# Batch 0's value loads without their blank rows, the softmax constant added on GpSimd, four plain float32 steps in place of five, and new due times, in a windowed attention with a gated mixing layer

## The chip, the cores and the metric

The kernel runs on one core of a Trainium2 chip. The metric is the device time of one launch in microseconds (us), the median of several runs. Engines are named as in the profile: PE multiplies matrices (TensorE, with PEld for its weight loads), DVE is VectorE, ACT is ScalarE, POOL is GpSimd, and SP (SyncE) issues nearly all DMAs. Each engine works through its own queue in order and waits on semaphores for the others.

## The reference

Inputs are q, k and v of shape (4 batches, 8 heads, 768 positions, 64) and the weights of a gated layer. Cut to what is computed:

```
scores_l = scale * q @ k^T            where |i - j| < 16, else -1e9
scores_s = scale * q @ max(k, blocks of 32) + log(32)
a = softmax(concat(scores_l, scores_s))   # sum gets + 1e-9
attn = a @ concat(v, mean(v, blocks of 32))
x = attn, heads side by side: (4, 768, 512); x_prev = x one position earlier
xk, xr = mu_k * x + (1 - mu_k) * x_prev, mu_r * x + (1 - mu_r) * x_prev
out = sigmoid(xr @ w_r) * (relu(xk @ w_k)^2 @ w_v)      # 512 -> 1024 -> 512
```

## The kernel before, in words

**Attention.** Heads are taken in pairs, so a batch has four pairs (`NPAIR`), and each pair is cut into two halves of 384 positions. One `unit` (L567) is a pair and a half. Queries are taken 64 at a time (12 windows, `NW`). A window sees 96 keys near it and the 24 block summaries: 120 columns (`NK`), in the order 64 near keys, 24 summaries (columns 64 to 87, `QW` to `KB`), 32 near keys. Scores are matmuls (L559). For each of six groups of 128 rows DVE adds the mask and finds the extreme (L585), ACT takes the exponential and the row sum (L589). DVE adds 1e-9 to the unit's six sums (L595) and takes the reciprocal (L596), and POOL multiplies the six groups by it (L601, "norm"). For batch 0 PE turns the weights round (L608) and ACT copies them out (L614). For later batches DVE and DMAs do it (L626, L635, L639). The product with the values is L656.

**Values.** `load_set` (L446) loads, for a pair, the keys (L452) and for each half a tile `vw` of 128 rows (L456): 64 rows of near values, 24 rows of zeros, 32 rows of near values, 8 rows of zeros, all laid out on the host. For batch 0, PE takes the block means out of these tiles (L490, the zero rows count for nothing in it), a second matmul puts them in place (L509), with ACT copies between (L508, L511), and the means are spread over rows 64 to 87 of both halves, by DVE or POOL (L515) and by a DMA on SP (L522). Later batches take their means by another way.

**The gated layer.** Its work per batch and half is a gate (L717 to L719, or L730 in plain float32 for the first half) and `experts` (L740), eight steps over 128 hidden features each. A step has a first product (L757), a relu and a square on ACT (L764, L766), and a second product (L784). A split step takes operands as a high and a low part, both in the fast matmul format, and adds three products: 12 matmuls of 384 columns in the first, 9 of 512 in the second. Its low and high parts come from a cast (`kh`, L770 on DVE or L771 on ACT) and a subtraction (`kl`, L772). A plain step multiplies float32 as it is: 4 matmuls and 3, each of which shows as two records. In the first half of batch 0 the first five steps are plain (`PLAIN = 5, 5`, L64), since the split weights aren't there yet. The weights are decoded from 64-bit words (L411, L414, L416) and split (L428 or L429, L433). The last batch uses a scheme with seven products in place of eight (L929, after L1020), with sums of weights (L848) that go out to memory and are fetched again.

**The order of the work.** `Plan` (L133) writes the order of every engine before the kernel runs. Each operation has a modelled length (`LENGTH`), its dependencies and a due time. `schedule` (L171) walks through time, gives each engine the ready operation that is due first, and models DMAs (`DMA_FIXED`, bytes) and the place that DVE and POOL share (`LOCKS`). Constants set the due times (`GATE0`, `STEP0`, `GATE1`, `PERIOD`, `STEP`), how far ahead things are loaded, and how PE is kept busy: where it would wait longer than `GAP`, a multiplication of zeros (`warm`, L439) is put in. The order is fixed when the kernel is built; on the chip each engine follows it and waits where the data is late. Weight combinations may not start before `AFTER` on the planner's clock.

The line that the change to the softmax sums touches is this:

```
def inverse():
    nc.vector.tensor_scalar_add(sm.t, sm.t, 1.0e-9)
    nc.vector.reciprocal(out=rc.t, in_=sm.t)
```

Of the kernel before, what the change touches and what calls it, by code (L numbers as in the profile page):

```python
# [13 lines left out]
ALU = mybir.AluOpType  # L14
# [3 lines left out]
B, H, S, D = 4, 8, 768, 64  # L18
DM, DF = 512, 1024
BLOCK, WINDOW = 32, 16  # L20
P = 128
NPAIR = H // 2
NS = S // BLOCK
QW = 64
NW = S // QW
LK = QW + 2 * WINDOW
NK = LK + NS
KB = QW + NS
KL = NW * KB + 2 * WINDOW
HW = NW // 2  # L30
NSL = HW // 2
# [8 lines left out]
LENGTH = dict(  # L40
    score=950, values2=1715, score2=1600, transpose=350, vturn=110, vpool=800, vsel=330, spread=540, spread_p=900, values=1020, gate=2740, gate32=930, e1=2100,
    e1_32=2690, e2a=1400, e2b=705, e2=705, e2_32=2600, e2l_32=930,
    warm=223, kred=865, kred2=470, kmax=90, kcopy=280, vred=865, mask=204, rc=320, evac=470, mixd=535, sub=475, khv=280,
    result=600, wbits=340, wor=610, wsub=605, tiny=60,
    exp=380, pts=375, vm=160, mixa=515, cast=405, relu=380, square=425, sigmoid=500, sigmoid3=1600, wscale=570, wcast=530,
    seven2=1040, seven4=2080, keep=375, keep_d=470, addp=600, sum=535, sum_p=900, relu2=805, relu2_d=620, result_t=500,
    tcast=530, comb3=1000, comb2=660, tsub=610, norm=345, wcast_p=640, mixa_p=600, kcopy_p=450, evac_a=375, flip=560,
)
TAIL = dict(PE=0, DVE=85, ACT=95, POOL=0, SP=0)
LATENCY = dict(PE=260, DVE=110, ACT=110, POOL=150, SP=0)  # L50
# [6 lines left out]
ATTENTION = "score", "score2", "values", "values2"  # L57
JOINED = 200
BOND = 0
DMA_FIXED = 2000  # L60
GATE0 = 32000
FULL = 34000
STEP0 = 5600
PLAIN = 5, 5  # L64
GATE1 = 80000
PERIOD = 52000
STEP = 4800
SLACK = 400
WARM = 260
WARM_END = 110000  # L70
GAP = 300
COLD = 5000
EARLY = 20000
AHEAD = 18000
ISSUE = 500
ISSUES = dict(const=0, put=460, get=400, spread=450)
HOLD = 900
LOOK = 500
LOOK_END = 60000
URGE = 5000  # L80
LOOKS = "PE",
AFTER = 100000
FLOATS = 8
AHEAD3 = 30000
SLACK3 = 200
LANES = 8
TABLE = 1300
TABLES = dict(sigmoid=1, sigmoid3=1, exp=0, wscale=0)
LOCKS = {"wbits", "wor", "wsub", "mixd", "sub", "kcopy", "khv", "spread", "sum", "tsub", "comb2", "comb3"}
FIRST = 4000  # L90
SECOND = 58000, 64000, 70000, 76000
FIRST_UNITS = 3500
FIRST_AHEAD = 14000
UNITS = 7500


class Slot:
# [35 lines left out]
class Plan:  # L133
# [10 lines left out]
    def op(self, eng, cost, due, emit, reads=(), writes=(), size=0, other=None):  # L144

        bufs = []
        for x, _ in list(reads) + list(writes):
            if isinstance(x, Buf) and x not in bufs:
                bufs.append(x)
        ways = {eng: (LENGTH.get(cost, 0), emit)}  # L150
        if other:
            ways[other[0]] = (LENGTH[other[1]], other[2])
        o = Op(len(self.ops), ways, due, bufs, size)
        for x in reads:
            o.deps.update(self.writers.get(x, ()))
        for x in writes:
            o.deps.update(self.writers.get(x, ()))
            o.deps.update(self.readers.get(x, ()))
        for x in reads:
            self.readers.setdefault(x, []).append(o)  # L160
        for x in writes:
            self.writers[x] = [o]
            self.readers[x] = []
        o.deps.discard(o)
        for x in bufs:
            x.users.append(o)
        self.ops.append(o)
        o.name = cost
        return o
# [139 lines left out]
def tile_kernel(ctx: ExitStack, tc: tile.TileContext, q, k, vT, v, consts, w_k, w_v, w_r, out):  # L309
# [136 lines left out]
    def load_set(b, p):  # L446
# [6 lines left out]
               writes=[(kt, f"k{n}")], size=P * (hi - lo) * 4)  # L453
        e["kparts"] = [(kt, f"k{n}") for n in range(len(cuts) - 1)]
        for hf in range(2):
            op("SP", "load", None, lambda hf=hf: nc.sync.dma_start(  # L456
                out=vw[hf].t[:, 0:S], in_=v[b, p, hf]),
               writes=[(vw[hf], "a"), (vw[hf], "b")], size=P * HW * 512)

        def blocks():  # L460
            return kt.t[:, 0:NW * KB].rearrange("p (j c) -> p j c", c=KB)
# [21 lines left out]
        if b == 0:  # L483
            tp = buf("mm", F32, False)

            def means():
                for i in range(3):
                    for g in range(4):
                        w = 3 * g + i
                        nc.tensor.matmul(  # L490
                            tp.t[32 * g:32 * g + 32, 0:P], pool_sb[:, 4 - 2 * i:36 - 2 * i],
                            windows(vw[w // HW])[:, w % HW, :], start=(i == 0), stop=(i == 2))

            op("PE", "vpool", None, means, reads=[(x, y) for x in vw for y in "ab"] + [*POOLM], writes=[(tp, 0)])
        else:
            vt, vs, vb, far = buf("st", U32), buf("vs"), buf("vb"), buf("farv")

            def tokens():
                return vt.t[:, 0:S].bitcast(F32)

            op("SP", "load", None, lambda: nc.sync.dma_start(out=tokens(), in_=vT[b - 1, p]), writes=[(vt, 0)], size=P * S * 4)
            op("DVE", "vred", None, lambda: nc.vector.tensor_reduce(
                out=vs.t[:, 0:NS], in_=tokens().rearrange("p (n c) -> p n c", c=BLOCK), op=ALU.add, axis=AX.X),
               reads=[(vt, 0)], writes=[(vs, 0)])
            op("DVE", "vturn", None, lambda: nc.vector.transpose(out=vb.t, in_=vs.t), reads=[(vs, 0)], writes=[(vb, 0)])
# [61 lines left out]
    def unit(b, p, hf, e, due):  # L567
# [23 lines left out]
                    accum_out=sm.t[:, NSL * h + i:NSL * h + i + 1]),  # L591
                   reads=[(y[h], i), (mn[h], i)], writes=[(y[h], i), (sm, NSL * h + i)])

        def inverse():
            nc.vector.tensor_scalar_add(sm.t, sm.t, 1.0e-9)  # L595
            nc.vector.reciprocal(out=rc.t, in_=sm.t)  # L596

        op("DVE", "rc", None, inverse, reads=[(sm, n) for n in range(2 * NSL)], writes=[(rc, 0)])
        for h in range(2):
            for i in range(NSL):  # L600
                op("POOL", "norm", None, lambda h=h, i=i: nc.gpsimd.tensor_scalar(  # L601
# [39 lines left out]
               reads=[(far, c) for c in range(4)], writes=spots, size=P * 3072)  # L641

        parts = e.setdefault("parts", [])
        parts.append((av, vw, pts, [(vw, x) for x in "ab"] + spots, hf))
        if b > 0 and hf == 0:
            return
        todo = list(parts)
# [555 lines left out]
```

## Time and profile before

| | |
|---|---|
| median of 3 runs | 418.39 us (418.35 to 419.38) |
| the profiled execution | 419.9 us, span of the core 417.9 us |
| granted clock of TensorE | 1.00 |
| DMA | 79.68 MB, 191 GB/s on the mean |
| first PE instruction to last | 0.99 to 414.6 us |

The span runs from the first instruction of the program to its last. A busy PE in these records isn't PE at its peak, since matmuls overlap and their ends are modelled; the pace is read from one start to the next, which the chain of work does. The time goes to the slowest engine of each stage, so the busy times are read by stretches.

### The profile page before, as it was taken

To read this page: it belongs to the slowest core of one execution; us is meant where nothing else is said; L and a number is where in the kernel's file an instruction comes from. 1 tells how busy PE (TensorE), PEld (TensorE's weight loads), DVE (VectorE), ACT (ScalarE), POOL (GpSimd) and SP (SyncE) were. 2 spreads that over 40 slices of the span, in tenths; PEclk is the share of its full clock that TensorE was granted. 3 is DMA by queue.
4 is the path that set the end of the run, shared out by engine and by line. 5 is a ranking of instruction groups with operands and counts; after the bars stand their busy time and mean duration, and the time that the engine had idled before them with its cause. 6 is when DMAs were issued, how large, how long until landed. Compare 5 with 4: busy or idle time off the path is not lost.

```text
span 417.9 us, 9808 instructions
## 1 busy us (share of the span) xinstructions
PE 411.0 (98%) x3363; PEld 349.6 (84%) x3363; DVE 344.6 (82%) x1053; ACT 286.8 (69%) x815; POOL 126.2 (30%) x255
## 2 busy tenths in 40 slices
PE   9999999999999999999999999999999999999996
PEld 8754556788888888988888889988889899999996
DVE  3879999999998699879798779569476598878993
ACT  2889999899874589537774459465595675669710
POOL 0471565534660033602353000422433030204100
PEclk9999999999999999999999999999999999999999
DMA  8995678678877585787735554486855314230012
GB/s 306 405 292 208 221 257 313 236 252 235 241 204 236 168 279 173 226 274 240 234 106 155 179 163 190 114 315 190 243 166 138 107 66 146 67 103 25 2 57 94
DMA packets 48193, 79.68 MB, mean 191 GB/s; under 512 B 6736, under 2 KB 28176, under 8 KB 48144
## 3 DMA queue, kind: packets, MB, share of 16 engines
q1 hardware_dynamic: 48000, 78.78, 58.3%
q8 instruction: 26, 0.43, 0.4%
q10 hardware_dynamic: 144, 0.28, 0.2%
q14 instruction: 23, 0.19, 0.2%
HBM read 58.68 MB, written 20.07 MB: 188 GB/s over the span
## 4 chain that ended last, share of the span: by engine, by line
PE 74%; ACT 9%; DVE 8%; DMA 5%; issue 2%; POOL 0%; SPq 0%; ACTq 0%; DVEq 0%; POOLq 0%
PE bank L784 20%; PE bank L757 19%; PE bank L929 14%; PE bank L1020 4%; PE bank L656 4%; PE bank L559 4%; ACT y L589 3%; DMA kt<-in_k 3%; PE bank L440 3%; PE bank L719 2%; PE bank L717 2%; PE bank L718 2%; DMA st<-in_w_k 2%; DVE wc L848 1%; DMA farw<-wc 1%
## 5 line engine op out<-in xcount | busy, mean ns | idle before, releaser
L601 POOL TENSOR_SCALAR y<-y,rc 128x120 f32<-128x120 f32 x192 | 93.8, 509 | 129.8 <-DVE mn L585 48.9
L757 PE MATMUL bank<-xs,w 128*128 128x384 f32 x556 | 112.0, 349 | 0.7 <-ACT z L708 0.5
L757 PEld LDWEIGHTS bank<-xs,w 128*128 128x128 f32 x556 | 98.1, 188 | 9.5 <-issue 1.0
L589 ACT ACTIVATE y<-y,mn 128x120 f32<-128x120 f32 x192 | 73.4, 385 | 15.3 <-DVE mn L585 15.0
L784 PE MATMUL bank<-w,kh 128*128 128x512 f32 x258 | 69.5, 397 | 0.4 <-DVE kh L770 0.4
L764 ACT ACTIVATE r<-bank 128x384 f32<-128x384 f32 x48 | 23.5, 490 | 50.2 <-PE bank L757 49.9
L784 PEld LDWEIGHTS bank<-w,kh 128*128 128x128 f32 x258 | 47.2, 188 | 9.5 <-DVE kh L770 0.7
L585 DVE CUSTOM_DVE_ANT_0 y<-bank,consts_sb 128x120 f32<-128x120 f32 x192 | 41.9, 272 | 0.1
L784 PE MATMUL bank<-w,kl 128*128 128x512 f32 x129 | 39.4, 398 | 0.0
L589 ACT ACTIVATION_READ_ACCUMULATOR y<-y,mn 128x1 f32 x192 | 36.4, 189 | 0.0
L656 PEld LDWEIGHTS bank<-pts,vx 120*64 120x64 f32 x768 | 24.0, 138 | 8.3 <-issue 6.8
L929 PE MATMUL bank<-xs,w 128*128 128x384 f32 x126 | 30.8, 337 | 0.0
L626 DVE STREAM_TRANSPOSE st<-y 128x384 f32<-128x384 f32 x48 | 27.0, 566 | 3.4 <-POOL y L601 2.8
L784 PEld LDWEIGHTS bank<-w,kl 128*128 128x128 f32 x129 | 23.8, 188 | 5.9 <-DVE kl L772 0.3
L770 DVE CAST kh<-r 128x384 fp32r<-128x384 f32 x26 | 9.7, 372 | 22.6 <-ACT r L766 22.6
L685 POOL TENSOR_SCALAR xa<-vx,om_sb 128x384 f32<-128x384 f32 x11 | 9.1, 832 | 62.6 <-DVE xs L699 62.6
L656 PE MATMUL bank<-pts,vx 120*64 120x64 f32 x768 | 26.8, 224 | 0.0
L772 DVE TENSOR_TENSOR kl<-r,kh 128x384 fp32r<-128x384 f32 x43 | 24.3, 565 | 2.2 <-ACT kh L771 0.8
L766 ACT ACTIVATE r<-r 128x384 f32<-128x384 f32 x48 | 25.3, 527 | 0.7
L559 PEld LDWEIGHTS bank<-kt,qt 64*64 64x64 f32 x768 | 19.9, 133 | 6.5 <-issue 3.4
L559 PE MATMUL bank<-kt,qt 64*64 64x120 f32 x768 | 24.7, 268 | 0.4 <-DVE kt L478 0.3
L697 ACT CAST xs<-xa 128x384 fp32r<-128x384 f32 x40 | 20.0, 510 | 6.9 <-DVE xa L688 6.9
(374 smaller groups left out, 832.2 us busy)
## 6 DMA issues: line engine op xcount, KB each, us to landing
vx<-in_v SPq DMA_DIRECT2D x32, 384.0 KB
far<-st SPq DMA_DIRECT2D x96, 96.0 KB
pts<-far SPq DMA_DIRECT2D x24, 384.0 KB
kt<-in_k SPq DMA_DIRECT2D x15, 544.0 KB
qt<-in_q SPq DMA_DIRECT2D x32, 192.0 KB
st<-in_vT SPq DMA_DIRECT2D x12, 384.0 KB
out<-z SPq DMA_DIRECT2D x18, 256.0 KB
st<-in_w_k SPq DMA_DIRECT2D x8, 512.0 KB
```

The source lines that it names most:

```text
L559: nc.tensor.matmul(cells(to[h])[cs, i, 0:NK], t.t[hs, n * QW:(n + 1) * QW], kt.t[hs, w * KB:w * KB + NK], start=True, stop=True)
L585: op("DVE", "mask", None, lambda h=h, i=i, var=var: nc.vector.tensor_tensor_reduce(out=cells(y[h])[:, i, 0:NK], in0=cells(spot[h])[:, i, 0 ...
L589: op("ACT", "exp", None, lambda h=h, i=i: nc.scalar.activation(cells(y[h])[:, i, 0:NK], cells(y[h])[:, i, 0:NK], AF.Exp, bias=mn[h].t[:, i ...
L601: op("POOL", "norm", None, lambda h=h, i=i: nc.gpsimd.tensor_scalar(out=cells(y[h])[:, i, 0:NK], in0=cells(y[h])[:, i, 0:NK], scalar1=rc.t ...
L626: op("DVE", "flip", due - (FIRST_AHEAD if b == 1 else AHEAD) + 8000 + 600 * h, lambda h=h: nc.vector.transpose(out=turned()[:, :, h], in_= ...
L656: nc.tensor.matmul(av.t[hs, w * QW:(w + 1) * QW], windows(vw)[:, w, hs], weights_of(pts)[0:NK, 2 * c:2 * c + 2, h, i], start=True, stop=True)
L757: nc.tensor.matmul(ps.t[:, 0:HT], w.t[:, p * P:(p + 1) * P], x[p][s].t, start=(n == 0), stop=(n == len(terms) * NPAIR - 1))
L764: op("ACT", "relu", None, lambda: nc.scalar.activation(r.t, ps.t[:, 0:HT], AF.Relu), reads=[(ps, 0)], writes=[(r, 0)])
L766: op("ACT", "square", None, lambda: nc.scalar.activation(r.t, r.t, AF.Square), reads=[(r, 0)], writes=[(r, 0)])
L772: op("DVE", "sub", None, lambda: nc.vector.tensor_tensor(out=kl.t, in0=r.t, in1=kh.t.bitcast(F32), op=ALU.subtract), reads=[(r, 0), (kh, 0 ...
L784: nc.tensor.matmul(acc[t].t, a.t[:, t * P:(t + 1) * P], v.bitcast(F32) if single else v, start=start, stop=stop)
L929: nc.tensor.matmul(bank.t[:, 0:HT], pair[w].t[:, col:col + P], a[k][s].t, start=(first and n == 0), stop=(n == 3 * nk - 1), skip_group_che ...
```

## The change

Four things are done together. First, for batch 0 the value loads leave out the 24 zero rows and the last 8: each half's load becomes two DMAs, of rows 0 to 63 and 88 to 119, and POOL writes zeros to rows 64 to 87 at the very start, since the block means still read them. The regions of the tile are now three ("a", "b", "c"). Later batches load as before. Second, adding 1e-9 to the softmax sums becomes an operation of its own on POOL ("eps"); DVE keeps the reciprocal. Third, `PLAIN` goes from 5, 5 to 4, 4: the fifth step of the first half is a split one, so its two weight tiles must be split before it, and the tile whose second-product weights are split last is the fourth. Fourth, some thirty constants of the planner change: due times, assumed DMA time, how far it looks ahead and on which engines, when zeros are multiplied, and when the weight combinations may start.

```diff
--- before.py
+++ after.py
@@ -40,11 +40,11 @@
 LENGTH = dict(
     score=950, values2=1715, score2=1600, transpose=350, vturn=110, vpool=800, vsel=330, spread=540, spread_p=900, values=1020, gate=2740, gate32=930, e1=2100,
     e1_32=2690, e2a=1400, e2b=705, e2=705, e2_32=2600, e2l_32=930,
-    warm=223, kred=865, kred2=470, kmax=90, kcopy=280, vred=865, mask=204, rc=320, evac=470, mixd=535, sub=475, khv=280,
+    warm=223, kred=865, kred2=470, kmax=90, kcopy=280, vred=865, mask=204, rc=160, eps=110, evac=470, mixd=535, sub=475, khv=280,
     result=600, wbits=340, wor=610, wsub=605, tiny=60,
     exp=380, pts=375, vm=160, mixa=515, cast=405, relu=380, square=425, sigmoid=500, sigmoid3=1600, wscale=570, wcast=530,
     seven2=1040, seven4=2080, keep=375, keep_d=470, addp=600, sum=535, sum_p=900, relu2=805, relu2_d=620, result_t=500,
-    tcast=530, comb3=1000, comb2=660, tsub=610, norm=345, wcast_p=640, mixa_p=600, kcopy_p=450, evac_a=375, flip=560,
+    tcast=530, comb3=1000, comb2=660, tsub=610, norm=345, blank=700, wcast_p=640, mixa_p=600, kcopy_p=450, evac_a=375, flip=560,
 )
 TAIL = dict(PE=0, DVE=85, ACT=95, POOL=0, SP=0)
 LATENCY = dict(PE=260, DVE=110, ACT=110, POOL=150, SP=0)
@@ -57,41 +57,41 @@
 ATTENTION = "score", "score2", "values", "values2"
 JOINED = 200
 BOND = 0
-DMA_FIXED = 2000
+DMA_FIXED = 2300
 GATE0 = 32000
 FULL = 34000
-STEP0 = 5600
-PLAIN = 5, 5
-GATE1 = 80000
-PERIOD = 52000
-STEP = 4800
-SLACK = 400
+STEP0 = 4400
+PLAIN = 4, 4
+GATE1 = 76000
+PERIOD = 51000
+STEP = 4400
+SLACK = 800
 WARM = 260
 WARM_END = 110000
-GAP = 300
+GAP = 500
 COLD = 5000
 EARLY = 20000
 AHEAD = 18000
 ISSUE = 500
 ISSUES = dict(const=0, put=460, get=400, spread=450)
-HOLD = 900
-LOOK = 500
-LOOK_END = 60000
-URGE = 5000
-LOOKS = "PE",
-AFTER = 100000
+HOLD = 600
+LOOK = 1000
+LOOK_END = 34000
+URGE = 2000
+LOOKS = "PE", "DVE", "ACT", "POOL"
+AFTER = 150000
 FLOATS = 8
-AHEAD3 = 30000
-SLACK3 = 200
+AHEAD3 = 20000
+SLACK3 = 100
 LANES = 8
 TABLE = 1300
 TABLES = dict(sigmoid=1, sigmoid3=1, exp=0, wscale=0)
 LOCKS = {"wbits", "wor", "wsub", "mixd", "sub", "kcopy", "khv", "spread", "sum", "tsub", "comb2", "comb3"}
-FIRST = 4000
+FIRST = 4500
 SECOND = 58000, 64000, 70000, 76000
-FIRST_UNITS = 3500
-FIRST_AHEAD = 14000
-UNITS = 7500
+FIRST_UNITS = 2500
+FIRST_AHEAD = 12000
+UNITS = 6500
 
 
 class Slot:
@@ -453,9 +453,16 @@
                writes=[(kt, f"k{n}")], size=P * (hi - lo) * 4)
         e["kparts"] = [(kt, f"k{n}") for n in range(len(cuts) - 1)]
         for hf in range(2):
+            if b == 0:
+                op("POOL", "blank", -1.0e5, lambda hf=hf: nc.gpsimd.memset(vw[hf].t[QW:KB, 0:S], 0.0), writes=[(vw[hf], "b")])
+                for part, lo, hi in ("a", 0, QW), ("c", KB, NK):
+                    op("SP", "load", None, lambda hf=hf, lo=lo, hi=hi: nc.sync.dma_start(
+                        out=vw[hf].t[lo:hi, 0:S], in_=v[b, p, hf, lo:hi]),
+                       writes=[(vw[hf], part)], size=(hi - lo) * HW * 512)
+                continue
             op("SP", "load", None, lambda hf=hf: nc.sync.dma_start(
                 out=vw[hf].t[:, 0:S], in_=v[b, p, hf]),
-               writes=[(vw[hf], "a"), (vw[hf], "b")], size=P * HW * 512)
+               writes=[(vw[hf], "a"), (vw[hf], "b"), (vw[hf], "c")], size=P * HW * 512)
 
         def blocks():
             return kt.t[:, 0:NW * KB].rearrange("p (j c) -> p j c", c=KB)
@@ -491,7 +498,7 @@
                             tp.t[32 * g:32 * g + 32, 0:P], pool_sb[:, 4 - 2 * i:36 - 2 * i],
                             windows(vw[w // HW])[:, w % HW, :], start=(i == 0), stop=(i == 2))
 
-            op("PE", "vpool", None, means, reads=[(x, y) for x in vw for y in "ab"] + [*POOLM], writes=[(tp, 0)])
+            op("PE", "vpool", None, means, reads=[(x, y) for x in vw for y in "abc"] + [*POOLM], writes=[(tp, 0)])
         else:
             vt, vs, vb, far = buf("st", U32), buf("vs"), buf("vb"), buf("farv")
 
@@ -591,11 +598,10 @@
                     accum_out=sm.t[:, NSL * h + i:NSL * h + i + 1]),
                    reads=[(y[h], i), (mn[h], i)], writes=[(y[h], i), (sm, NSL * h + i)])
 
-        def inverse():
-            nc.vector.tensor_scalar_add(sm.t, sm.t, 1.0e-9)
-            nc.vector.reciprocal(out=rc.t, in_=sm.t)
-
-        op("DVE", "rc", None, inverse, reads=[(sm, n) for n in range(2 * NSL)], writes=[(rc, 0)])
+        sums = [(sm, n) for n in range(2 * NSL)]
+        op("POOL", "eps", None, lambda: nc.gpsimd.tensor_scalar(
+            out=sm.t, in0=sm.t, scalar1=1.0e-9, scalar2=1.0, op0=ALU.add, op1=ALU.mult), reads=sums, writes=sums)
+        op("DVE", "rc", None, lambda: nc.vector.reciprocal(out=rc.t, in_=sm.t), reads=sums, writes=[(rc, 0)])
         for h in range(2):
             for i in range(NSL):
                 op("POOL", "norm", None, lambda h=h, i=i: nc.gpsimd.tensor_scalar(
@@ -641,7 +647,7 @@
                reads=[(far, c) for c in range(4)], writes=spots, size=P * 3072)
 
         parts = e.setdefault("parts", [])
-        parts.append((av, vw, pts, [(vw, x) for x in "ab"] + spots, hf))
+        parts.append((av, vw, pts, [(vw, x) for x in "abc"] + spots, hf))
         if b > 0 and hf == 0:
             return
         todo = list(parts)
```

## The prediction

> **What bounds the kernel now.** I read the page first, for the busy time of each engine, then the busy time by stages, because the averages hide that the stages have different limits.
>
> ```profile
> span 417.9 us, 9808 instructions
> PE 411.0 (98%) x3363; PEld 349.6 (84%) x3363; DVE 344.6 (82%) x1053; ACT 286.8 (69%) x815; POOL 126.2 (30%) x255
> vx<-in_v SPq DMA_DIRECT2D x32, 384.0 KB
> ```
>
> ```profile
> 8.00:20.00 12.00, 11.70 (x207) 9.20 (x199) 10.19 (x57) 9.68 (x40) 4.24 (x14) 1.00 1.03 406
> 20.00:30.00 10.00, 9.55 (x120) 5.46 (x120) 8.22 (x28) 8.25 (x30) 7.17 (x13) 1.00 0.97 298
> 30.00:40.00 10.00, 9.58 (x69) 4.67 (x68) 8.91 (x20) 9.14 (x19) 2.25 (x3) 1.00 0.71 259
> 40.00:60.00 20.00, 19.64 (x124) 10.93 (x124) 19.53 (x56) 19.94 (x54) 11.96 (x14) 1.00 0.58 204
> 60.00:110.00 50.00, 49.49 (x462) 37.77 (x462) 48.92 (x187) 47.00 (x150) 22.43 (x49) 1.00 0.83 266
> 110.00:160.00 50.00, 49.50 (x454) 42.66 (x458) 43.55 (x144) 33.82 (x105) 18.46 (x37) 1.00 0.69 210
> 160.00:340.00 180.00, 180.00 (x1481) 158.02 (x1474) 141.46 (x450) 116.62 (x336) 49.41 (x106) 1.00 0.59 185
> 340.00:417.90 77.90, 74.56 (x425) 74.06 (x423) 62.08 (x115) 41.08 (x89) 9.52 (x10) 1.00 0.23 75
> ```
>
> The columns are the stretch, its length, then PE, PEld, DVE, ACT and POOL busy, the granted clock (1.00 throughout), the busy share of the DMA engines and GB/s. PE is the bound: from 160 to 340 us it is busy 180.00 of 180.00. But its busy time holds filler. The timeline of PE shows it at the start (L440 multiplies zeros by zeros and gives nothing):
>
> ```profile
> 0.99 6.61 PE L440 MATMUL bank<-zero_sb 128*128 128x128 f32 x32 [0.99 <-POOL zero_sb L1066]
> 7.53 0.85 PE L559 MATMUL bank<-kt,qt 64*64 64x120 f32 x24
> 8.31 2.50 PE L440 MATMUL bank<-zero_sb 128*128 128x128 f32 x20
> ...
> 12.30 0.94 PE L440 MATMUL bank<-zero_sb 128*128 128x128 f32 x6
> ...
> 13.88 0.83 PE L440 MATMUL bank<-zero_sb 128*128 128x128 f32 x6
> ...
> 19.51 0.49 PE L440 MATMUL bank<-zero_sb 128*128 128x128 f32 x2
> ```
>
> So four kinds of PE time can shrink. Work: steps that can be made cheaper. Filler: 6.61 us before the first scores, and 2.50 + 0.94 + 0.83 + 0.49 = 4.8 us after them. Idle time between 8 and 160 us: 0.30 + 0.45 + 0.42 + 0.36 + 0.51 + 0.50 = 2.5 us. And the tail: in the last row 77.90 - 74.56 = 3.3 us, which no edit touches. Beyond the work, then, 4.8 + 2.5 = 7.3 us can be won at the very most once the scores have begun. DVE and ACT are nearly full from 40 to 110 us (19.53 and 19.94 of 20, 48.92 and 47.00 of 50); there a later DVE is a later PE.
>
> **Four plain steps in place of five.** The chain of work that ended last has both kinds of step:
>
> ```profile
> 52.72 2.58 PE bank L784 x6
> ...
> 62.93 2.58 PE bank L757 x8
> ...
> 167.55 2.10 PE bank L757 x12
> 169.65 2.08 PE bank L784 x9
> ```
>
> A plain float32 step is 2.58 us (first matrix, 4 matmuls of two records) and 2.58 us (second). A split step is 2.10 and 2.08. The fifth step changes kind: 5.16 - 4.18 = **-0.98 us** of PE work, which counts in full, since PE has nothing to hide it behind. Its price lies on DVE and ACT:
>
> ```profile
> L433 DVE TENSOR_TENSOR w<-w,w 128x512 fp32r<-128x512 f32 x19 | 13.7, 733 | 0.0
> L770 DVE CAST kh<-r 128x384 fp32r<-128x384 f32 x26 | 9.7, 372 | 22.6 <-ACT r L766 22.6
> L772 DVE TENSOR_TENSOR kl<-r,kh 128x384 fp32r<-128x384 f32 x43 | 24.3, 565 | 2.2 <-ACT kh L771 0.8
> L595 DVE TENSOR_SCALAR sm<-sm 128x6 f32<-128x6 f32 x32 | 5.3, 167 | 3.0 <-ACT y L589 2.8
> L596 DVE RECIPROCAL rc<-sm 128x6 f32<-128x6 f32 x32 | 6.1, 192 | 1.1
> ```
>
> New work is one kh and one kl: 0.37 + 0.57 = 0.94 us of DVE. The two splits of the fifth weight tiles (L433, 2 x 0.73 us, and their casts) are no new work, they only come some steps sooner, in the stage where DVE is full. What hides this is the saving of the next part; without it, up to 0.94 + 1.47 = 2.4 us would be late at PE's fifth step.
>
> **The constant on GpSimd.** L595 leaves DVE. The timeline of DVE shows what one costs, and the pair of units to which the second rival below refers:
>
> ```profile
> 6.14 0.31 DVE L478 COPY kt<-ks 128x288 f32<-128x288 f32 x1
> ...
> 11.63 0.17 DVE L595 TENSOR_SCALAR sm<-sm 128x6 f32<-128x6 f32 x1 [1.04 <-ACT y L589]
> 11.84 0.19 DVE L596 RECIPROCAL rc<-sm 128x6 f32<-128x6 f32 x1
> ...
> 43.54 0.15 DVE L595 TENSOR_SCALAR sm<-sm 128x6 f32<-128x6 f32 x1
> ...
> 89.86 0.16 DVE L595 TENSOR_SCALAR sm<-sm 128x6 f32<-128x6 f32 x1
> ...
> 91.70 0.26 DVE L595 TENSOR_SCALAR sm<-sm 128x6 f32<-128x6 f32 x1
> ...
> 107.82 0.17 DVE L595 TENSOR_SCALAR sm<-sm 128x6 f32<-128x6 f32 x1
> ```
>
> From its start to that of the reciprocal it is 11.84 - 11.63 = 0.21 us, 32 times: 6.7 us off DVE in all. Nine of the 32 lie between 40 and 110 us, the first at 43.54 and the last at 107.82: 1.9 us, twice the 0.94 that the fifth step adds. The eps goes from ACT to POOL to DVE to POOL where it went ACT, DVE, DVE, POOL. On POOL it costs between the smallest memset and a norm over 120 columns:
>
> ```profile
> 0.73 0.20 POOL L1066 MEMSET zero_sb<- 128x128 f32 x1 [0.29 <-POOLq L1191]
> 0.87 0.11 POOL L1068 MEMSET vs<- 128x8 f32 x1
> ...
> 12.22 2.08 POOL L601 TENSOR_SCALAR y<-y,rc 128x120 f32<-128x120 f32 x6 [10.97 <-DVE mn L585]
> ```
>
> That is 0.11 to 2.08 / 6 = 0.35 us; I take 0.15, since six columns are nearest to the 128x8 row. The new wait is DVE's: its reciprocal now waits for POOL, and behind it in DVE's queue stand the masks, kl and xs that ACT and PE want. In time for PE I take **-0.3 us**, out of the 0.36 + 0.51 us idle from 40 to 110; the bounds are -0.9 and, as a rival, plus.
>
> **Batch 0's values.** Each of the 8 loads moves 96 rows of 128 and becomes two DMAs. From 8 to 20 us the DMA engines are full at 406 GB/s, so a load of 384 KB takes 0.97 us and by its bytes would take 0.73: 8 x 0.24 = 1.9 us less queue when the last has landed. The nearest row is the load itself, as its rows keep their length. The far end comes from the one narrow copy at the front, 24 rows, 72 KB:
>
> ```profile
> L522 SPq DMA_DIRECT2D vx<-vm x4: 822/827/972, 17.6 to 31.4; - x4
> ```
>
> In the stretch from 20 to 30 us, which holds most of them, the engines are just as full but move 298 GB/s: 1.08 MB less than at 406, or 2.7 us, so 0.67 us for each even if all four lay there, where their bytes would make 0.18. Were each of the two new pieces to take as long as a whole load, the queue would be 8 x 0.97 = 7.8 us later. I take -1.9 for the queue. Little of it can reach PE: in SP's order of issues the keys and queries of pairs 0 and 1 come ahead of any value; the keys of pair 2 stand behind two of these loads (-0.5), those of pair 3 behind four (-1.0), the last weights behind all. With 4.8 us of filler to draw on, I count half, **-1.0 us** (0 to -1.9).
>
> The Trainium skill speaks against this edit: SBUF — State Buffer, section "Door 1: The DMA port swizzle", has a transfer over partitions 0 to 63 reach 8 of 16 ports, at 196 GB/s where 128 partitions got 328. By its figures a pair of pieces would be an estimated 1.5 us instead of 0.97, the queue 4 us later and not 1.9 sooner. By that rule, the 24-row copies (0.67 us or more for 72 KB) agree in direction, but their pieces are short; no row has a 64-partition load.
>
> The eight extra issues cost SP about 0.43 us each (3.4 us before 20 us):
>
> ```profile
> L456 SPq DMA_DIRECT2D vx<-in_v x32: 327/430/1222, 3.1 to 303.6; - x32
> ```
>
> I cost them at nothing: what stands behind them on SP's queue, keys, queries and gate weights, would join a full DMA queue. The eight memsets of 24 x 768 go first on POOL. By the two memset rows (0.20 us for 128 columns, 0.11 for 8) a column is 0.75 ns, so one is about 0.68 us, all 5.5 us, over at about 6.5. POOL's next work is at 12.22, so that hides them; should they hold DVE's L478 of 6.14 to 6.45 until 6.5, the first scores at 7.53 still have a microsecond in hand.
>
> **New due times.** They change the order on all queues. PE's work is the same in any order; what can go is waiting. From 160 to 340 us there is none. Delaying the weight combinations (AFTER) takes DVE work out of 110 to 150 us, where PE was idle 0.50 us, and puts it after 150, where DVE has 38 of 180 us free. I take **-0.3 us**; the bounds are -1.9 (the 2.2 us of idle time from 20 to 160 us but for the 0.3 counted above) and a few us more, as any reordering can make a new wait.
>
> **The sum.** -0.98 - 1.0 - 0.3 - 0.3 = -2.6 us. The profiled execution took 419.9 us for a span of 417.9, so 417.3 for it; the median, 418.39, lies 1.5 below that execution, which gives **415.8 us** (0.6% faster). About 0.3%, or 1.26 us, is what a measurement of this kernel can tell from no change: 417.1 to 419.7.
>
> **The rivals.** First, that only the work counts: the filler and the waits stay because ACT and DVE, at 9.68 and 10.19 of 12 us in the stage from 8 to 20, set the front and not the DMA. Then -0.98 remains: 417.4, no change that can be told. For it speaks that the first scores start straight after filler, not after a wait.
>
> Second, the slower side by the loads: narrow pieces at half the rate. A 64-row piece takes what 128 rows take, 0.97 us, a 32-row piece 0.48: 0.48 more for each load, 3.9 us at the end of the eight. Pair 3's values, then its mix and the last gate products wait; PE has 0.45 + 0.42 us of idle time from 20 to 40 that this would replace, so 3.0 us come on top of -0.98 - 0.6: 419.8. It is slower by over 0.3% from about 0.46 us more for each load. The short 24-row copies are all in the trace that supports it. This is what the Trainium skill's rule above would do.
>
> Third, DVE waits for the eps. In a pair of units such as that of 89.86 and 91.70 us the second eps may stand behind the first unit's six norms on POOL:
>
> ```profile
> L601 POOL TENSOR_SCALAR y<-y,rc 128x120 f32<-128x120 f32 x192 | 93.8, 509 | 129.8 <-DVE mn L585 48.9
> POOL y L601 <- DVE rc L596: 42.2, 12, 11.1
> ```
>
> Six take 6 x 0.509 = 3.05 us, the units are 1.84 apart, so DVE would wait 1.2 us, in the four pairs of batch 1 where DVE is full 4.9 us: 418.39 - 0.98 - 1.0 + 4.9 = 421.3. Against it: POOL itself mostly sits waiting for the reciprocal (42.2 us in 12 waits), so the eps usually finds it free.
>
> **How the numbers follow.** Forecast 0.64, only the work 0.20, narrow loads 0.09, queued eps 0.07. The forecast's low end takes the whole 1.9 of the queue and all 2.5 us of idle time: 418.39 - 0.98 - 1.9 - 2.5 = 413.0. The range reaches up past the narrow loads to 420.0 and leaves out the queued eps. Faster 0.64, same 0.20, slower 0.09 + 0.07 = 0.16.
>
> **What would show it.** The plain steps: L757 in pieces x8 four times, not five. The loads: the stage from 8 to 20 us still at about 400 GB/s, gate weights landing 1 to 2 us sooner, filler after 8 us below 4 us; a rate near 300 GB/s there means the narrow loads. The eps: DVE's reciprocal with no wait for POOL over 0.3 us, DVE's busy time down by about 4 us (5.3 less 0.94). PE's idle time from 20 to 160 us at or below 2.2 us. A single new PE wait of over 2 us in any stage, or 3 us more filler, would make the forecast wrong.

## The result and the profile after

Slower, and outside the range on the other side: 423.68 us (421.22 to 425.93, 6 runs) against 418.72 us (418.35 to 419.47, 6 runs), a ratio of 1.011 with a 95% interval of 1.007 to 1.015. The profiled execution of after took 421.99 us, 2.1 us more than that of before (419.9) and less than most of the timed runs of after; that spread is taken up again below.

The page of after, its span, engines and the DMA issues of the values:

```profile
span 419.9 us, 9858 instructions
PE 408.8 (97%) x3362; PEld 349.7 (83%) x3362; DVE 335.6 (80%) x1020; ACT 288.2 (69%) x818; POOL 137.4 (33%) x297
...
vx<-in_v SPq DMA_DIRECT2D x24, 384.0 KB
...
vx<-in_v SPq DMA_DIRECT2D x8, 192.0 KB
vx<-in_v SPq DMA_DIRECT2D x8, 96.0 KB
```

Batch 0's eight loads have become 8 of 192 KB and 8 of 96 KB, as the change says. VectorE (DVE) has 9.0 us less to do and GpSimd (POOL) 11.2 us more. TensorE (PE) is busy 2.2 us less and the span is 2.0 us longer, so it waits more. The stages show where (columns as in the prediction: busy time of PE, PEld, DVE, ACT, POOL, then granted clock, DMA share, GB/s):

```profile
8.00:20.00 12.00, 8.75 (x148) 6.58 (x148) 7.88 (x44) 5.99 (x29) 3.46 (x11) 1.00 1.04 275
20.00:30.00 10.00, 8.81 (x117) 5.42 (x115) 7.02 (x30) 8.02 (x33) 5.11 (x13) 1.00 1.05 247
30.00:40.00 10.00, 9.04 (x95) 4.74 (x94) 7.49 (x14) 8.13 (x17) 7.12 (x12) 1.00 0.91 296
40.00:60.00 20.00, 19.67 (x118) 10.12 (x117) 19.62 (x57) 19.86 (x53) 8.66 (x11) 1.00 0.64 222
60.00:110.00 50.00, 49.23 (x454) 39.14 (x453) 46.84 (x159) 42.72 (x128) 24.65 (x48) 1.00 0.76 254
```

From 8 to 20 us the DMA engines are as full as before (1.04) and move 275 GB/s where they moved 406. PE is busy 8.75 of 12 us where it was 11.70, DVE 7.88 where it was 10.19, ACT 5.99 where it was 9.68: everyone waits for data. From 8 to 40 us PE is now idle 3.25 + 1.19 + 0.96 = 5.4 us where it was 0.30 + 0.45 + 0.42 = 1.2. PE's timeline at the front and its waits name what is late:

```profile
8.70 0.84 PE L566 MATMUL bank<-kt,qt 64*64 64x120 f32 x24 [0.98 <-DVE kg L477]
9.47 1.16 PE L440 MATMUL bank<-zero_sb 128*128 128x128 f32 x8
11.23 1.18 PE L497 MATMUL bank<-vx,consts_sb 120*32 120x128 f32 x24 [0.60 <-DMA vx<-in_v]
12.34 0.94 PE L440 MATMUL bank<-zero_sb 128*128 128x128 f32 x6
14.51 0.85 PE L566 MATMUL bank<-kt,qt 64*64 64x120 f32 x24 [1.24 <-DVE kg L477]
...
16.38 1.25 PE L497 MATMUL bank<-vx,consts_sb 120*32 120x128 f32 x24 [0.69 <-DMA vx<-in_v]
...
22.74 0.38 PE L497 MATMUL bank<-vx,consts_sb 120*32 120x128 f32 x3 [0.78 <-DMA vx<-in_v]
```

The block means (L497, L490 before) wait for values three times. The scores (L566) wait twice, and the view names VectorE's work on keys (L477) for it; but the second of these runs until 14.56 us, past the start of the scores at 14.51. The semaphores of the trace have the queries of these scores land at 8.56 and 14.42 us, just before they start. In the kernel with whole loads of the first experiment below the same queries land at 7.49 and 11.33. In the order of both kernels the second pair's queries stand behind the first pair's values. What PE lost from 0 to 40 us (the time between starts less the usual pace of that work, filler of zeros counted as lost) rose from 14.9 to 19.3 us, +4.4. After 40 us it fell by 1.5, and the work itself by 1.0; together that is +1.9, and the span is 2.0 longer.

The mean of 275 GB/s hides two rates. This is the view of DMA over 4 to 30 us, in 40 slices of 0.65 us, first of after, then of a kernel that differs from it only in loading whole tiles again (the first experiment):

```profile
GB/s 397 345 368 354 319 189 217 264 225 226 364 367 207 182 235 252 247 345 335 414 396 303 195 180 233 266 273 384 336 210 202 241 225 262 251 235 225 165 150 289
```

```profile
GB/s 429 417 380 394 428 402 443 410 391 398 392 416 433 427 382 408 382 387 399 406 410 399 394 395 416 418 395 372 272 179 216 321 162 91 202 422 365 143 192 347
```

After's row falls again and again to between 180 and 230 and comes back to some 350 to 400 in between; the other stays near 400 until 22 us. The valleys are where the values pass: in steps of 0.2 us in which nothing but values moved, the trace has 185 to 231 GB/s in after and 395 to 417 with whole loads. The last of batch 0's values landed at 29.5 us in after, at 25.6 in before and at 24.75 in the kernel with whole loads.

### The profile page after: what moved, and what is told of

It is laid out like the page before. It is cut to its first block, busy times and chain, and to the rows that moved or that the text cites. A ratio compares the mean times of both kernels' runs of the same rounds, so it can differ in the third digit from the quotient of the medians.

```text
span 419.9 us, 9858 instructions
## 1 busy us (share of the span) xinstructions
PE 408.8 (97%) x3362; PEld 349.7 (83%) x3362; DVE 335.6 (80%) x1020; ACT 288.2 (69%) x818; POOL 137.4 (33%) x297
## 4 chain that ended last, share of the span: by engine, by line
PE 77%; DMA 9%; ACT 6%; DVE 5%; issue 1%; SPq 1%; DVEq 0%; ACTq 0%
PE bank L790 22%; PE bank L763 21%; PE bank L935 14%; PE bank L662 4%; PE bank L1026 4%; PE bank L566 3%; PE bank L723 3%; PE bank L724 3%; PE bank L725 3%; DMA st<-in_w_r 2%; ACT y L596 2%; DMA vx<-in_v 2%; DMA kt<-in_k 2%; DMA st<-in_w_k 1%; DMA qt<-in_q 1%
## 5 line engine op out<-in xcount | busy, mean ns | idle before, releaser
L607 POOL TENSOR_SCALAR y<-y,rc 128x120 f32<-128x120 f32 x192 | 91.7, 496 | 21.6 <-DVE rc L604 15.3
L790 PE MATMUL bank<-w,kh 128*128 128x512 f32 x264 | 71.4, 398 | 0.8 <-DVE kh L776 0.8
L790 PEld LDWEIGHTS bank<-w,kh 128*128 128x128 f32 x264 | 48.1, 188 | 10.7 <-DVE kh L776 1.0
L602 POOL TENSOR_SCALAR sm<-sm 128x6 f32<-128x6 f32 x32 | 8.8, 276 | 111.6 <-ACT y L596 109.7
L632 DVE STREAM_TRANSPOSE st<-y 128x384 f32<-128x384 f32 x48 | 27.2, 570 | 10.3 <-POOL y L607 10.3
L566 PEld LDWEIGHTS bank<-kt,qt 64*64 64x64 f32 x768 | 19.8, 133 | 8.5 <-issue 3.1
L566 PE MATMUL bank<-kt,qt 64*64 64x120 f32 x768 | 24.3, 268 | 2.2 <-DVE kg L477 2.2
L473 DVE TENSOR_REDUCE kg<-kt 128x48 f32<-128x768 f32 (+1 forms) x17 | 15.3, 899 | 13.9 <-DMA kt<-in_k 13.8
```

Of the source, the lines that this page charges most:

```text
L566: nc.tensor.matmul(cells(to[h])[cs, i, 0:NK], t.t[hs, n * QW:(n + 1) * QW], kt.t[hs, w * KB:w * KB + NK], start=True, stop=True)
L632: op("DVE", "flip", due - (FIRST_AHEAD if b == 1 else AHEAD) + 8000 + 600 * h, lambda h=h: nc.vector.transpose(out=turned()[:, :, h], in_= ...
L790: nc.tensor.matmul(acc[t].t, a.t[:, t * P:(t + 1) * P], v.bitcast(F32) if single else v, start=start, stop=stop)
```

## The experiments

**One: after with whole loads (whole_in_after).** The order on every queue stays that of after; only the loads are whole again, and the memsets are gone.

```diff
-op("POOL", "blank", ..., lambda hf=hf: nc.gpsimd.memset(vw[hf].t[QW:KB, 0:S], 0.0), ...)
+op("POOL", "blank", ..., lambda: None, ...)
-    nc.sync.dma_start(out=vw[hf].t[lo:hi, 0:S], in_=v[b, p, hf, lo:hi]),   # parts "a" and "c"
+    part == "a" and nc.sync.dma_start(out=vw[hf].t[:, 0:S], in_=v[b, p, hf]),
```

> The changed kernel in its own order on every queue, but each of batch 0's eight value loads is one DMA of all 128 rows again and the eight memsets are gone. Theory (loads that span part of the partitions move at about half the rate): from 8 to 20 us the DMA engines return from 275 to about 400 GB/s, PE's idle time from 8 to 40 us falls from 5.4 us to under 2.5, and the time falls by 3 to 5 us, to 419 to 420. Rival (the new due times made the front late, as the first scores' queries now stand behind the next pair's keys; the loads matter little): still slower than before by 1%, 423, first scores still at about 8.7 us and idle time still over 4 us.

Measured: 417.16 us, ratio to before 0.994 (0.991 to 0.996), the fastest kernel of the study. The time is lower than expected (419 to 420). So the loads and their memsets cost after about 1.7%, and the rest of the change, in this order, gains 0.6%. No run has the memsets without the split loads, so their own share stays open. Its front:

```profile
8.00:20.00 12.00, 9.88 (x179) 7.53 (x177) 9.29 (x53) 7.71 (x37) 5.13 (x14) 1.00 1.04 405
20.00:30.00 10.00, 9.22 (x129) 5.26 (x129) 7.95 (x26) 9.46 (x32) 6.82 (x16) 1.00 0.87 276
30.00:40.00 10.00, 10.00 (x90) 5.18 (x86) 9.06 (x23) 8.83 (x19) 5.40 (x7) 1.00 0.87 281
```

405 GB/s again, and PE idle 2.9 us from 8 to 40 where after has 5.4; under 2.5 was expected.

**Two: the loads alone, in before (narrow_in_before).** Before's order, each of batch 0's value loads as rows 0 to 63 and 88 to 119, the eight memsets at the start.

```diff
+def values_in(hf=hf):
+    for lo, hi in ((0, QW), (KB, NK)) if b == 0 else ((0, P),):
+        nc.sync.dma_start(out=vw[hf].t[lo:hi, 0:S], in_=v[b, p, hf, lo:hi])
```

> The kernel before in its own order, but each of batch 0's value loads is two DMAs of rows 0 to 63 and 88 to 119 and the rows between are set to zero by eight memsets at the start. Theory: 8 to 20 us at about 280 GB/s, the last value load lands about 4 us later, time 421 to 423. Rival (due times): 417 to 418.7, since fewer bytes are moved.

Measured: 424.32 us (419.78 to 427.81), ratio 1.013 (1.010 to 1.017). Without the two longest of the six runs the median is 423.96, 1.0% above before. The loads and memsets alone cost in before's order about what all of after costs. The profiled execution was the fastest of the six (419.78); even there the stage from 8 to 20 us ran at 313 GB/s, and the last value landed 2.2 us later than in before, where about 280 GB/s and 4 us were expected.

**Three and four: two loads of 128 rows, or two of 64 (two_by_columns, two_by_rows).** Both double the number of value loads of batch 0 in before and leave the bytes as they are. One cuts each load by columns, the other by rows.

```diff
+for lo, hi in ((0, HT), (HT, S)):                 # two_by_columns
+    nc.sync.dma_start(out=vw[hf].t[:, lo:hi], in_=v[b, p, hf, :, lo:hi])
+for lo, hi in ((0, QW), (QW, P)):                 # two_by_rows
+    nc.sync.dma_start(out=vw[hf].t[lo:hi, 0:S], in_=v[b, p, hf, lo:hi])
```

> The kernel before, with each of batch 0's value loads cut into two DMAs by columns: 128 rows each, half the row. Same bytes, eight more DMAs. Theory (the span of partitions counts): as before, 418.0 to 419.0, 8 to 20 us at 390 GB/s or more. Rival (each DMA has its cost, whatever its shape): slower like the narrow loads, 421 or more, rate about 300 GB/s.

> The kernel before, with each of batch 0's value loads cut into two DMAs by rows: 0 to 63 and 64 to 127. Same bytes, eight more DMAs, no memsets. Theory: each half takes about as long as the whole did (0.97 us), so the queue is up to 7.8 us later after the eight, 8 to 20 us at 230 to 260 GB/s, time 423 to 427. Rival (bytes and number of DMAs count): the same as the cut by columns.

Measured: 419.70 us, ratio 1.000 (0.998 to 1.002), and 427.48 us, ratio 1.018 (1.015 to 1.022). The stage from 8 to 20 us, by columns and then by rows:

```profile
8.00:20.00 12.00, 10.15 (x173) 7.82 (x175) 9.41 (x55) 8.56 (x37) 4.24 (x14) 1.00 1.05 396
```

```profile
8.00:20.00 12.00, 9.19 (x143) 6.88 (x143) 6.84 (x44) 7.40 (x34) 4.24 (x14) 1.00 1.04 290
```

The same bytes in as many pieces run at 396 or at 290 GB/s, by how many partitions a piece spans (230 to 260 was expected for the cut by rows). Neither the number of issues nor a fixed cost of each piece can be the cause. This is the rule of the Trainium skill that the prediction cited against the edit. Another section of the same page of the Trainium skill (SBUF — State Buffer, "Can I just issue two DMAs to hit both halves?") says that a transfer below partition 64 and one above it run one after the other and hardly side by side. Two_by_rows agrees with it: its last values landed at 34.4 us, those of two_by_columns at 27.2.

**Five: zeros where PE waits (zeros_in_after).** After's timed runs lie up to 4 us above its profiled one, and several show a granted clock of 0.992 to 0.996. I thought that PE, idle at the front, loses its clock in most runs. This kernel puts 20 more multiplications of zeros into PE's queue, at the five waits shown above and ahead of one more score.

```diff
+for _ in range(3 if p in (1, 2) else 0):          # ahead of the block means
+    nc.tensor.matmul(tp.t[:, 512 - P:512], zero_sb, zero_sb, start=True, stop=True)
+for _ in range(extra.get(o, 0)):                  # 4 ahead of three scores, 2 ahead of the first means
+    o.emit()                                      # o: a multiplication of zeros
```

> The kernel after, with some 18 more multiplications of zeros at the front of TensorE's queue, at the five places where it waited for batch 0's keys and values (0.6 to 1.2 us each). They can't make any data come sooner. Theory A, the idle TensorE at the front costs granted clock in most runs, and that makes up what the timed runs lie above the profiled one (421.2 to 425.9 us at 0.992 to 1.000): the clock is 0.999 or 1.000 in every run, the runs lie within 1.5 us of each other, and the median is near 421.5. Theory B, the late data alone do it: the clock may rise, but the median stays at 423 to 424.5 and the runs spread over 4 us.

Measured: 425.32 us (421.01 to 428.33). The clock was 0.999 or 1.000 in five of six runs, and the time was no shorter and no steadier. My theory of the clock fell. Its profiled execution took 425.46 us at a clock of 0.999, and shows what differs:

```profile
8.00:20.00 12.00, 10.05 (x147) 8.31 (x146) 7.18 (x36) 5.66 (x28) 2.57 (x8) 1.00 1.05 261
20.00:30.00 10.00, 8.85 (x128) 5.98 (x126) 6.25 (x34) 4.64 (x19) 5.76 (x15) 1.00 1.01 220
```

261 and 220 GB/s, where the profiled execution of after had 275 and 247; PE's busy time there is padded by the zeros, DVE and ACT show the waiting. Across the profiled executions time goes with the landing of the last of batch 0's values:

| kernel | last value landed, us | profiled execution, us |
|---|---|---|
| whole_in_after | 24.75 | 417.6 |
| before | 25.6 | 419.9 |
| two_by_columns | 27.2 | 419.8 |
| narrow_in_before | 27.8 | 419.8 |
| after | 29.5 | 422.0 |
| zeros_in_after | 32.0 | 425.5 |
| two_by_rows | 34.4 | 428.3 |

Each row is one execution, and two orders are mixed here. In before's order (before, two_by_columns, narrow_in_before, two_by_rows) a landing up to 27.8 us costs nothing that shows, and the 6.6 us from there to two_by_rows cost 8.5, of which up to 1.7 are a fall of PE's clock (last section). In after's order the first 4.7 us already cost 4.4, and the next 2.5 cost 3.5. That the loads' rate varies from run to run and makes the spread of after is what this table suggests; the timed runs have no trace to show it.

**Six to nine: the other edits, each with an order of its own.** Each of these is a kernel in which the planner writes the order anew.

```diff
+PLAIN = 4, 4                          # plain4_only: before with this alone
+op("POOL", "eps", ...); rc=160, eps=110   # eps_only: before with the constant on GpSimd, its lengths
+op("SP", "load", ..., size=P * HW * 512)   # all_but_loads: after with before's value loads
+PLAIN = 5, 5; GATE1 = 76000; ...      # due_times_only: before with after's other constants
```

> The kernel before with four plain steps in place of five and nothing else changed; the planner writes its order anew with the old constants. Theory (the work term counts in full): 0.98 us less PE work, ratio 0.9965 to 0.9985, PE's idle time from 40 to 110 us within 0.5 us of the 0.87 of before. Rival (DVE, full from 40 to 110 us, gives it back): ratio 0.9985 or more, idle time there over 1.5 us.

> The kernel before with the constant of the softmax sums on GpSimd and nothing else changed. Theory (hidden): ratio 0.997 to 1.001, DVE's busy time down by 5 us. Rival (DVE waits for the eps behind other norms): ratio over 1.003 and waits of PE on DVE of over 1 us between 40 and 160 us.

> The changed kernel without its edit of the value loads: one DMA of 128 rows each, no memsets; eps, four plain steps and the new constants stay, and the planner writes the order anew. Theory (narrow loads are the whole loss): ratio 0.990 to 0.996, rate from 8 to 20 us about 400 GB/s, no run with a granted clock under 0.996. Rival (the new order is fragile at the front in itself): ratio 0.999 or more.

> The kernel before with the new planner constants alone: five plain steps, whole loads, the sums as before. Theory (the order after the front got better, PE's lost time after 40 us fell by 1.5 us in the changed kernel): ratio 0.994 to 0.998. Rival (my forecast of -0.3 us): 0.998 to 1.001. Third (queries behind keys cost a microsecond at the start): over 1.001, first scores after 8 us.

| kernel | median, us | ratio, 95% |
|---|---|---|
| plain4_only | 425.81 | 1.015 (1.013 to 1.018) |
| eps_only | 431.42 | 1.028 (1.025 to 1.031) |
| all_but_loads | 426.58 | 1.017 (1.014 to 1.020) |
| due_times_only | 418.98 | 0.999 (0.997 to 1.000) |

I had not expected the first three; the fourth fits the forecast for the due times, no change that can be told. All_but_loads does the very work of whole_in_after; only the order differs, since the planner counted whole loads in the one and narrow ones in the other. (The order includes which of two engines takes some of the copies, and how many multiplications of zeros are put in.) The order alone is worth 2.4%, 9 us, more than any edit here. Where 4.4 of the 9 us go, first all_but_loads, then whole_in_after:

```profile
100.00:110.00 10.00, 8.49 (x109) 7.51 (x102) 7.71 (x42) 8.14 (x33) 4.47 (x12) 1.00 0.72 185
...
160.00:340.00 180.00, 176.56 (x1461) 153.21 (x1461) 143.89 (x456) 119.49 (x341) 55.77 (x127) 1.00 0.64 195
```

```profile
100.00:110.00 10.00, 9.46 (x91) 8.56 (x90) 8.10 (x46) 9.99 (x43) 6.28 (x17) 1.00 0.78 208
...
160.00:340.00 180.00, 180.00 (x1445) 158.35 (x1444) 146.30 (x452) 122.67 (x346) 48.89 (x114) 1.00 0.65 197
```

PE waits at the handover to batch 1 and, in all_but_loads, it waits 3.4 us in the long stage where before and whole_in_after have no wait at all. Plain4_only loses at the same handover; its PE there, line numbers as in before:

```profile
102.19 0.97 PE L757 MATMUL bank<-xs,w 128*128 128x384 f32 x4 [0.85 <-ACT xs L697]
...
109.60 1.66 PE L784 MATMUL bank<-w,kh 128*128 128x512 f32 x6 [1.20 <-ACT kh L771]
...
114.19 0.92 PE L656 MATMUL bank<-pts,vx 120*64 120x64 f32 x24 [0.82 <-DVE mn L585]
```

Step after step waits a little for ACT or DVE, which are busy 9.87 and 9.76 of the 10 us from 100 to 110.

**Ten to sixteen: the edit or the order?** Two kernels move the constant and keep the order: to GpSimd in before, and back to VectorE in whole_in_after.

```diff
-nc.vector.tensor_scalar_add(sm.t, sm.t, 1.0e-9)                      # eps_in_order; eps_back reverses it
+nc.gpsimd.tensor_scalar(out=sm.t, in0=sm.t, scalar1=1.0e-9, scalar2=1.0, op0=ALU.add, op1=ALU.mult)
```

> The kernel before with its own written order on every queue; only the 32 additions of the constant go from VectorE to GpSimd, each just ahead of where the reciprocal stood. Theory A, the move by itself costs nothing that counts (a GpSimd step of about 0.25 us off the path, 32 x 0.167 us off VectorE): 418.0 to 419.5, ratio 0.998 to 1.001, and the 2.8% that the same edit cost with a rewritten order came from the order. Theory B, the forecast's gain: 417.7 to 418.1 or less. Theory C, the second rival on the slower side (VectorE waits behind GpSimd's six norms): over 421, with VectorE's reciprocal waiting over 1 us in the pairs of units.

> The kernel after in its own order with whole value loads (416.0 to 418.7 us, ratio 0.994), and the addition of the constant back on VectorE at the place that the order gives it. If the move is worth nothing, the ratio stays at 0.992 to 0.996. If the move carries the gain of that order (VectorE is full from 40 to 110 us), it goes up to 0.997 or more. If the move costs in that order (the added wait of VectorE for GpSimd), it falls below 0.992.

Measured: 420.66 us, ratio 1.004 (1.002 to 1.005), and 417.80 us, ratio 0.996 (0.995 to 0.998). In before's order the move costs 0.4%, between what its first and third theory expected. DVE does wait for GpSimd there, as its waits show (us in total, times, the longest):

```profile
DVE rc L596 <- POOL sm L595: 9.4, 14, 1.3
```

In after's order, with room left for it, the same wait is 1.8 us in all (below), and taking the move back gained nothing: 0.996 against 0.994, with intervals that overlap, on two chips.

Four kernels write the order once more with one modelled length raised by 5 ns (`relu=385` for 380): before itself, and the three slow ones.

> The kernel before with one modelled length of the planner raised by 5 ns (a relu on ScalarE, 380 to 385): no instruction is added or removed, only the order on the queues is written anew. Theory A, the order of before is one of few good ones, and whatever makes the planner rewrite it costs 1 to 3%, as the three single edits did: 422 to 430 us. Theory B, those edits are slow in themselves (the split fifth step wants VectorE where it is full, the eps wants GpSimd): 418.0 to 420.0.

> The kernel before with four plain steps in place of five, as in the run that took 425.81 us, but the order written a second time, with one modelled length raised by 5 ns. Theory A, what that run lost (7.2 us between 100 and 130 us, in waits for ScalarE and VectorE) belongs to its order: the second order lies elsewhere, 417.5 to 423 us or above 427, with no such loss at the same place. Theory B, the split fifth step itself makes VectorE late there: 424.5 to 427 us again, and again 5 us or more lost from 100 to 130.

> The kernel before with the constant added on GpSimd, as in the run that took 431.42 us, but the order written a second time, with one modelled length raised by 5 ns. With its order held the move cost 0.4%. Theory A, the rest of the 2.8% belongs to the order: the second order is 419 to 427 us. Theory B, the move makes every newly written order slow: 429.5 to 433 us.

> The kernel after with before's value loads, order written anew, as in the run that took 426.58 us (span 424.8), but written a second time, with one modelled length raised by 5 ns. The same edits in after's own order took 417.2 us. Theory A, the 9 us between the two are the order's: the second one lies somewhere between, 417 to 424 us or above 428. Theory B, the narrow loads' modelled lengths (fewer bytes) are what lets the planner write the good order: 425 to 428 us again.

| kernel | first order, us | second order, us (ratio) |
|---|---|---|
| before | 419.18 | null_replan 419.74 (1.001) |
| plain4_only | 425.81 | plain4_again 432.05 (1.031) |
| eps_only | 431.42 | eps_again 423.45 (1.010) |
| all_but_loads | 426.58 | rest_again 426.55 (1.016) |

Two orders of one edit lie 6 and 8 us apart in two cases, so an order's luck is as large as the losses; in the third they agree. In the two slowest of these kernels part of the loss is PE's clock: in the profiled executions of eps_only and plain4_again it fell to half twice, for 10.2 us in all, which is up to 5 us of work (their timed runs have 0.987 to 0.996). The second order of plain4_only also waits at the same handover: PE is busy 6.81 of the 10 us from 100 to 110, where the first order has 7.55, so the split fifth step may be late there in itself. But a new order without an edit cost nothing, twice (null_replan, due_times_only), and all six with one edit alone, or without the loads, cost 1 to 3%. So the order decides here by microseconds, and what part of the 1 to 3% each edit would keep in a good order isn't settled by these.

The last kernel takes whole_in_after and issues the first pair's queries ahead of the second pair's keys, as before did, with five zero multiplications fewer.

```diff
+order[i], order[j] = order[j], order[i]      # SP: queries of pair 0, then keys of pair 1
+for o in zeros[-5:]: order.remove(o)
```

> The kernel after in its own order with whole value loads (ratio 0.994), its first pair's queries issued ahead of the second pair's keys, as before had it, and five zero multiplications fewer ahead of the first scores. Theory A, the front follows the first scores: they start near 6.9 us in place of 8.09, and the time falls by 0.6 to 1.2 us, ratio 0.990 to 0.992. Theory B, the later keys and values set the front (pair 3's keys landed at 16.1): the first scores come sooner and nothing else, ratio 0.993 to 0.995.

Measured: 418.09 us, ratio 0.997 (0.996 to 0.999). The first scores start at 6.51 us in place of 8.09, and the span is 415.6 us in place of 415.5. Starting earlier brought nothing: by 60 us PE had lost some 16 us in both kernels.

## Why the prediction was wrong

**Where it failed.** The step is "I take -1.9 for the queue". It took bytes for time: 96 rows of 128 as three quarters of 0.97 us. It was to bring -1.0 us on PE; after against whole_in_after, the split loads and memsets cost some 1.7%, or 7 us. The pieces run at about half the rate, and the eight loads ended 29.5 - 25.6 = 3.9 us later. The second rival worked out 3.9 us too, with a chance of 0.09; its mechanism was right, but that the figures agree to the tenth is luck. With the order held the same change made them end 4.7 us later (after against whole_in_after) and 2.2 us later (narrow_in_before against before). I wrote myself that no row has a load of 64 partitions, and then took the end of the range that follows from rows of 128. The one partial transfer in the trace, by my estimate 0.67 us or more for 72 KB, stood against it, and so did the Trainium skill's rule; I set both aside because the pieces are short.

**What the rival missed.** It priced those 3.9 us at 3.0 on PE and came to 419.8. PE's loss at the front was +4.4 in the profiled execution, because not only the last weights wait: the means of pairs 0, 1 and 2 and the queries of pairs 0 and 1 are each late in turn, and DVE and ACT run dry with them. That "the keys and queries of pairs 0 and 1 come ahead of any value" was read from before's order; in the new one pair 1's queries do not. The timed runs lie another 1.7 us higher by the median.

**Right in kind.** "A rate near 300 GB/s there means the narrow loads" named the sign: 275. The plain steps did what was said: PE's work, by the counts and paces of the prediction, fell by 0.98 us, and the chain of waits of after shows its plain pieces from 48 us on, the first step running from 44.80:

```profile
48.65 2.85 PE bank L763 x8
...
55.05 2.58 PE bank L763 x8
...
60.20 2.58 PE bank L763 x8
```

Four with the one that began at 44.80, where there were five. Work, constant and due times together were to bring -0.98 - 0.3 - 0.3 = -1.6 us; whole_in_after, which is after without the load edit, measured -2.5 against the before of its batch (419.66). The due times alone gave a ratio of 0.999 (0.997 to 1.000). Of the other signs, PE's idle time from 20 to 160 us was 3.3 us, not 2.2 or less, and VectorE's busy time fell by 9.0 us, not by about 4.

**The constant.** Its groups in after, with GpSimd's memsets and VectorE's reciprocal (busy us, mean ns, then the idle time before and its cause):

```profile
L602 POOL TENSOR_SCALAR sm<-sm 128x6 f32<-128x6 f32 x32 | 8.8, 276 | 111.6 <-ACT y L596 109.7 <-DVE ks L481 1.0
L457 POOL MEMSET vx<- 24x768 f32 x8 | 5.8, 753 | 0.2
...
L604 DVE RECIPROCAL rc<-sm 128x6 f32<-128x6 f32 x32 | 5.5, 174 | 1.8 <-POOL sm L602 1.8
```

I took 0.15 us and it is 0.28, nearer to the norm's 0.35 than to the memset by its columns. "No wait for POOL over 0.3 us" failed: DVE waits 1.8 us in three waits here, the longest 1.0, and 9.4 us in 14 waits in before's order, the longest 1.3, where the third rival had said 1.2. That rival's mechanism is real; its price, 4.9 us, was 1.5 in before's order.

**The memsets.** 5.8 us against 5.5 foreseen; but GpSimd took other small memsets between them and ended at 7.44 us, not 6.5, and they did hold the copy that the prediction named (L485, L478 before):

```profile
5.96 0.81 DVE L485 COPY kt<-ks 128x288 f32<-128x288 f32 x1
```

0.81 us in place of 0.31, which whole_in_after has again. "The first scores still have a microsecond in hand" held by another road than I meant: queries_first moved the first scores by 1.6 us with no effect on the span.

**The due times.** "A few us more, as any reordering can make a new wait" was the right bound and the wrong weight: orders of the same work differed by up to 9 us.

## What to carry to other kernels

Count a load by the partitions that it spans before its bytes: leaving out a quarter of the rows made eight loads end 4.7 us later in the same order, because transfers of 128 rows became transfers of 64 and 32. Where a trace has no row for such a transfer, the nearest partial load and a rule that says the opposite of the bytes deserve more than one chance in ten. Where a planner writes the order, an edit is measured with its order: keep the order fixed to learn the price of an edit, and write it more than once before you blame the edit.

## What the runs showed of the hardware

Loads of 64 and 32 partitions moved at about half the rate of loads of 128: 180 to 230 GB/s in the valleys against some 400. The Trainium skill's page SBUF — State Buffer gives 196 and 328 in "Door 1: The DMA port swizzle"; the narrow rate agrees, the wide one here is higher, with many loads queued. The narrow rate is unsteady: the stage from 8 to 20 us ran at 313, 290, 275 and 261 GB/s in four kernels with split rows, two of which issue the same loads in the same order.

The granted clock can fall in mid-kernel after short waits. In eps_only PE waited 2.7 us near 101 us, and the clock of the next stretches was (stretch, length, engines, then clock)

```profile
102.00:104.00 2.00, 0.31 (x2) 0.31 (x3) 1.67 (x8) 2.00 (x10) 0.00 (x0) 1.00 0.62 127
104.00:106.00 2.00, 2.00 (x9) 1.85 (x7) 1.82 (x15) 2.00 (x12) 0.73 (x3) 0.60 0.38 80
106.00:108.00 2.00, 2.00 (x40) 1.71 (x41) 1.93 (x6) 1.99 (x9) 2.00 (x4) 0.54 0.85 244
108.00:110.00 2.00, 2.00 (x29) 1.84 (x22) 1.93 (x6) 1.88 (x2) 1.26 (x3) 1.00 0.88 232
```

The two middle rows hold one stretch of 3.4 us, from 104.4 to 107.8, at a clock of 0.50, so about 1.7 us of work are lost on top of the wait. Two_by_rows shows the same, 0.50 from 24.6 to 28.0 us, after a wait of 2.3 us. In eps_only the clock is 0.50 once more from 152.2 to 159.0 us, after a wait of 2.1 us. The Trainium skill, TensorE: Matmul & The Clock Gate, "Part 1: The HAM clock gate", has the half rate come after an idle window of about 3.4 us that runs freely; here waits of 2.3 and 2.7 us were enough, with PE busy 1.71 and 1.26 of the 4 us around them. Many shorter waits did not do it: plain4_only had PE busy 7.55 of 10 us from 100 to 110 at a clock of 1.00.
